# A state-space and Fourier kernel: angles reduced to one turn at the parameters, an exponential of degree 6, and six of its steps on ScalarE

## The chip, the cores and the metric

The kernel runs on one core of a Trainium2 chip. The engines are called as the profile calls them: PE (TensorE, with PEld for its weight loads), DVE (VectorE), ACT (ScalarE), POOL (GpSimd) and SP (SyncE, which issues most transfers). The metric is the device time of one execution in microseconds (us).

## The reference

Two independent layers are computed from fp32 inputs and laid side by side. A is a Fourier mixing layer, written as matrix products. B is a diagonal state-space layer: a kernel of 2048 taps is built from exponentials of complex numbers and convolved with the input by Fourier transforms of twice the length.

```python
# A: x is 2048 x 512
a = einsum("bsd,ed->bse", x, dft_hid_re)
b = einsum("bsd,ed->bse", x, dft_hid_im)
y = einsum("ts,bse->bte", dft_seq_re, a) - einsum("ts,bse->bte", dft_seq_im, b)
# B: u is 2048 x 512, N = 128 states for each of 512 channels
dt = exp(log_dt)
A = -exp(log_A_real) + 1j * A_imag
C = (C_real + 1j * C_imag) * dt[:, None]
P = exp((A * dt[:, None])[:, :, None] * pos[None, None, :])
K = 2.0 * einsum("dn,dnl->dl", C, P).real
y = irfft(rfft(u, 2L) * rfft(K, 2L), 2L)[:L] + u * D_skip
```

## The kernel before

All work is written as small processes (Python generators) that ask a planner for time on an engine, by `yield "dve", cost`, and then record their instructions. The planner simulates the engines with these costs and so sets, when the kernel is built, the one order in which each engine's instructions stand. On the chip each engine takes its list in that order and waits at an instruction whose data or buffer is not ready.

Layer A (class `Fnet`) is the bulk of PE's list. Each fp32 tile of 128 x 512 is split in two, a rounded part (`hi`, line 229, on ACT) and the rest (`lo`, line 234, on DVE), and three matmuls (line 378) make up one product; an item of the list is such a tile with its 12 matmuls. At the start the tiles of x are split too (`x_hi`, `x_lo`). So PE needs one instruction of ACT and one of DVE for every new tile, two of each for the first sixteen items.

Layer B (class `Ssm`) is spread between these matmuls. Channels go in 16 blocks of `CHUNK` = 32:

- `setup` and `setup_rest` make the parameters of the first 128 channels and of the other 384. Each calls `exp` (an exponential from plain DVE instructions: clamp, reduce by a multiple of ln 2, a Horner polynomial, and a power of two made by writing (k + 127) * 2^23 as an integer), and then `params`, which multiplies by dt. `par[:, 1]` is the angle of one step in turns. The first call works in tiles named `cs`, the second in tiles named `t`; the parameters lie in `xk_sb`.
- `seed_args` makes 11 seeds of a block: the exponent and the angle times 1, 2, 4, ... 1024 (lines 659 and 661, ACT), the angle rounded to whole turns (663, ACT) and reduced (665, DVE), clamped to half a turn (667, DVE), its absolute value (669, ACT), and an exponential and three sines on ACT with two loads of ACT's function tables (671 to 677).
- `seeds`, `tables1` and `tables2` turn them into tables of powers by complex products on DVE (lines 616, 625, 639, 645, with squares on ACT in line 632), the longest share of DVE's list. A block's `taps` are matmuls (line 812).
- `stage1_k` (line 861) and `stage1_u` (line 916) are first stages of the transforms of taps and input; their results leave PSUM through ACT and DVE (lines 846 to 850 and 926 to 930). `product` (1040, 1067) multiplies the spectra and starts the inverse, and `inverse` and `inverse2` (1161, 1139) end it.

Layer B's matmuls use two PSUM tiles called `f`, each handed on only when ACT and DVE have emptied it. The next `seed_args` starts when the one before is done, so its steps stand spread over the whole time of a block.

Of the kernel before, what the change touches and what calls it, by code (L numbers as in the profile page):

```python
# [10 lines left out]
I32 = mybir.dt.int32  # L11
AF = mybir.ActivationFunctionType
OP = mybir.AluOpType
# [5 lines left out]
RND = 1.5 * 2.0 ** 23  # L19
TWO_PI = 6.283185  # L20
LN2_HI = 0.693359375
LN2_LO = 0.693147180559945309 - LN2_HI


def fft_constants():
# [162 lines left out]
def act(cols):  # L188
    return 0.09 + cols * 0.00085


def dve(cols, rate=1.0):
    return (66 + cols / rate) / 960


def load(kb, rate=330):
    return max(0.55, kb / rate)
# [241 lines left out]
class Ssm:  # L439
# [63 lines left out]
    def exp(self, x, k, f, p):  # L503

        n = math.prod(x.shape[1:])
        v = self.nc.vector
        yield "dve", dve(n, 2)
        v.tensor_scalar(x, x, -87.0, 88.0, op0=OP.max, op1=OP.min)
        yield "dve", dve(n, 2)
        v.tensor_scalar(k, x, 1.0 / math.log(2.0), RND, op0=OP.mult, op1=OP.add)  # L510
        yield "dve", dve(n, 2)
        v.tensor_scalar(k, k, RND, None, op0=OP.subtract)
        yield "dve", dve(n)
        v.scalar_tensor_tensor(f, k, -LN2_HI, x, op0=OP.mult, op1=OP.add)
        yield "dve", dve(n)
        v.scalar_tensor_tensor(f, k, -LN2_LO, f, op0=OP.mult, op1=OP.add)
        yield "dve", dve(n, 2)
        v.tensor_scalar(p, f, 1.0 / 5040, None, op0=OP.mult)
        for c in (1.0 / 720, 1.0 / 120, 1.0 / 24, 1.0 / 6, 0.5, 1.0):
            yield "dve", dve(n)  # L520
            v.scalar_tensor_tensor(p, p, c, f, op0=OP.add, op1=OP.mult)
        yield "dve", dve(n, 2)
        v.tensor_scalar(f.bitcast(I32), k, 127.0, 2.0 ** 23, op0=OP.add, op1=OP.mult)
        yield "dve", dve(n)
        v.scalar_tensor_tensor(x, p, 1.0, f, op0=OP.add, op1=OP.mult)

# [28 lines left out]
            nc.sync.dma_start(self.all[:, i, FIRST:], self.nd[i, :, FIRST:])  # L555
        self.plan.set(self.in2_ev)

    def params(self, par, alpha, dt):

        v = self.nc.vector  # L560
        n = par.shape[2]
        yield "dve", dve(n), *APART
        v.tensor_tensor(par[:, 0], alpha, dt, op=OP.mult)
        yield "dve", dve(n), *APART
        v.scalar_tensor_tensor(par[:, 1], par[:, 1], 1.0 / (2 * math.pi), dt, op0=OP.mult, op1=OP.mult)
        yield "dve", dve(n), *APART
        v.tensor_tensor(par[:, 2], par[:, 2], dt, op=OP.mult)
        yield "dve", dve(n), *APART
        v.scalar_tensor_tensor(par[:, 3], par[:, 3], -1.0, dt, op0=OP.mult, op1=OP.mult)

    def setup(self):
        yield self.in_ev
        yield from self.exp(*self.tmp)
        x = self.tmp[0]
        self.plan.spawn(self.spread_dt(x[:, 2 * FIRST:]), 0)
        yield self.in1_ev
        yield from self.params(self.all[:, :, :FIRST], x[:, FIRST:2 * FIRST], x[:, :FIRST])

    def spread_dt(self, dt):

# [8 lines left out]
    def setup_rest(self):  # L589
        yield self.in2_ev  # L590
        dt, *t = self.tmp2
        par = self.all[:, :, FIRST:]
        yield from self.exp(par[:, 0], *t)
        yield self.dt_ev
        yield from self.params(par, par[:, 0], dt)
        self.plan.put(self.t1s)
        yield "dma", load(900)
        self.nc.sync.dma_start(self.par_dram, par)
        self.plan.set(self.par_ev)
# [47 lines left out]
    def seed_args(self, ck, box, ev):  # L647

        a, v = self.nc.scalar, self.nc.vector
        if CHUNK * ck >= FIRST:  # L650
            yield from self.load_par(ck)
        par = self.par[ck]
        yield self.res
        s = self.tab.tile([128, 3, 11, CHUNK], F32, name="seed")
        args = s[:, 0:3:2]
        e, k, r = (s[:, n] for n in range(3))
        n = 11 * CHUNK
        yield "act", act(2 * n) + 4 * act(0)
        a.activation(args[:, :, 0], par[:, 0:2], AF.Copy)
        for j in (1, 2, 4, 8):  # L660
            a.activation(args[:, :, j:min(2 * j, 11)], args[:, :, 0:min(j, 11 - j)], AF.Copy, scale=2.0 ** j)
        yield "act", act(n)
        a.activation(k, r, AF.Copy, bias=RND)
        yield "dve", dve(n)
        v.scalar_tensor_tensor(r, k, RND, r, op0=OP.subtract, op1=OP.subtract)
        yield "dve", dve(n, 2)
        v.tensor_scalar(r, r, 0.5, -0.5, op0=OP.min, op1=OP.max)
        yield "act", act(n)
        a.activation(k, r, AF.Abs)
        yield "act", act(n) + 1.3  # L670
        a.activation(e, e, AF.Exp, scale=-1.0)
        yield "act", act(6 * CHUNK) + 1.4
        a.activation(r[:, 0:6], r[:, 0:6], AF.Sin, scale=-TWO_PI)
        yield "act", act(5 * CHUNK)
        a.activation(r[:, 6:11], r[:, 6:11], AF.Sin, scale=TWO_PI)
        yield "act", act(n)
        a.activation(k, k, AF.Sin, scale=-TWO_PI, bias=self.halfpi)
        box.append(s)
        self.plan.set(ev)
# [494 lines left out]
CHUNK, FIRST, JOIN = 32, 128, 0  # L1174
# [79 lines left out]
```

## Time and profile before

| | |
|---|---|
| Median of 3 runs | 578.7 us (577.9 to 579.09) |
| Profiled execution, its own time | 577.28 us |
| Its span, first to last instruction | 575.5 us |
| ACT's splits (line 229) waiting for PE's matmuls | 52.0 us in 39 waits |
| DVE's splits (line 234) waiting for ACT's | 23.8 us in 14 waits |
| ACT table loads | 32, of 1.28 us |
| DMA moved | 133.70 MB, 232 GB/s |

The granted TensorE clock is at its full value in all slices of the span. The page's busy time of PE is of little use by itself, because matmuls overlap: a row of line 378 lasts some 0.39 us while the next one starts 0.23 us after it. So PE is read by the steps between starts, and a group of matmuls of one line (a burst) by its whole length. DVE's rows overlap by less, some 0.08 us.

### The profile page before, as it was taken

The page shows a single profiled execution, that of the slowest core. Times are in us where ns is not written, and L with a number is a line of the kernel's source. Part 1 is how long each engine was busy: PE and PEld are TensorE (multiplying, and loading weights), DVE is VectorE, ACT ScalarE, POOL GpSimd, SP SyncE. Part 2 cuts the span into 40 slices and gives each one's busy share as a digit, 9 for nine tenths or more (in the row PEclk, how much of TensorE's full clock was granted, in tenths as well). Part 3 has the DMA queues.
Part 4 walks back from the last instruction along what each step waited for, and adds up shares of the span by engine and source line. Part 5 has one row for each costly group of instructions (what it writes and reads, how often), then busy time and mean ns, then how long its engine had stood idle before and what let it go on. Part 6 is the DMA issues. An engine that isn't in the chain of part 4 may idle for free.

```text
span 575.5 us, 15666 instructions
## 1 busy us (share of the span) xinstructions
PE 567.4 (99%) x6278; PEld 433.0 (75%) x6278; DVE 522.5 (91%) x927; ACT 371.4 (65%) x728; POOL 40.2 (7%) x60
## 2 busy tenths in 40 slices
PE   8999999999999999999999999999999999999997
PEld 6777777788777777778787777777687778776685
DVE  7999999999999999999999999999998999547732
ACT  5779665663777495758669576754588845355623
POOL 0000000000110000100100100001100000000000
PEclk9999999999999999999999999999999999999999
DMA  8998999997459767866697889559998897599984
GB/s 272 325 372 256 280 286 276 283 278 179 128 156 234 193 179 232 202 165 220 171 259 211 221 202 259 137 153 254 293 298 239 225 294 227 131 281 266 274 233 147
DMA packets 147976, 133.70 MB, mean 232 GB/s; under 512 B 47296, under 2 KB 107328, under 8 KB 147648
## 3 DMA queue, kind: packets, MB, share of 16 engines
q1 hardware_dynamic: 138976, 115.54, 66.6%
q0 software_dynamic: 8064, 14.68, 12.7%
q10 hardware_dynamic: 864, 2.49, 1.8%
q8 instruction: 49, 0.80, 0.6%
q14 instruction: 23, 0.19, 0.1%
HBM read 89.95 MB, written 42.73 MB: 231 GB/s over the span
## 4 chain that ended last, share of the span: by engine, by line
PE 56%; DVE 34%; issue 6%; ACT 2%; DMA 1%; DVEq 0%; ACTq 0%
PE acc L378 45%; DVE prod L616 12%; DVE t L625 7%; DVE lo L234 5%; PE f L1040 3%; PE f L812 2%; PE f L1067 2%; DVE t L645 2%; PE f L916 2%; DVE cs L686 1%; DVE z L1024 1%; DVE uk L1026 1%; DVE t L639 1%; DVE xk_sb L848 1%; PE f L1139 1%
## 5 line engine op out<-in xcount | busy, mean ns | idle before, releaser
L378 PE MATMUL acc<-hi,x_hi 128*128 128x512 f32 x640 | 258.0, 403 | 0.0
L378 PE MATMUL acc<-lo,x_hi 128*128 128x512 f32 x640 | 250.2, 391 | 0.0
L378 PE MATMUL acc<-hi,x_lo 128*128 128x512 f32 x640 | 249.6, 390 | 0.0
L616 DVE TENSOR_TENSOR prod<-t,cs 128x1024 f32<-128x1024 f32 (+4 forms) x192 | 163.0, 867 | 1.7 <-ACT t L734 0.6
L378 PEld LDWEIGHTS acc<-hi,x_hi 128*128 128x128 f32 x640 | 120.2, 188 | 49.1 <-issue 23.8
L378 PEld LDWEIGHTS acc<-hi,x_lo 128*128 128x128 f32 x640 | 120.3, 188 | 26.0
L378 PEld LDWEIGHTS acc<-lo,x_hi 128*128 128x128 f32 x640 | 120.4, 188 | 23.0 <-DVE lo L234 0.2
L229 ACT ACTIVATE hi<-raw 128x512 fp32r<-128x512 f32 x132 | 82.6, 628 | 67.7 <-PE acc L378 52.0
L234 DVE TENSOR_TENSOR lo<-raw,hi 128x512 fp32r<-128x512 f32 x132 | 90.0, 684 | 23.9 <-ACT hi L229 23.8
L625 DVE TENSOR_TENSOR t<-prod 128x512 f32<-128x512 f32 (+4 forms) x192 | 94.1, 511 | 1.0
L632 ACT ACTIVATE square<-t 128x256 f32<-128x256 f32 (+1 forms) x64 | 36.7, 574 | 31.5 <-DVE t L625 28.9
L332 POOL DMA_DIRECT2D lo<-in_sT x28 | 24.3, 868 | 216.0 <-ACT lo L330 40.4
L1019 ACT ACTIVATE uk<-f 128x1024 f32<-128x1024 f32 x32 | 31.1, 1017 | 10.4 <-PE f L1040 7.5
L812 PEld LDWEIGHTS f<-t,t 128*32 128x32 f32 x2048 | 29.5, 110 | 7.2 <-issue 5.1
L399 ACT ACTIVATE y<-acc 128x512 f32<-128x512 f32 x47 | 27.9, 595 | 10.6 <-PE acc L378 10.5
L812 PE MATMUL f<-t,t 128*32 128x64 f32 x2048 | 32.4, 220 | 1.2 <-issue 0.7
L327 POOL DMA_DIRECT2D hi<-in_sT x28 | 16.1, 576 | 186.1 <-PE acc L378 147.6
L1024 DVE TENSOR_TENSOR z<-uk 128x512 f32<-128x512 f32 x32 | 21.9, 684 | 4.4 <-ACT uk L1019 2.9
L1082 ACT ACTIVATE z<-f 128x512 f32<-128x512 f32 x32 | 17.7, 592 | 11.6 <-PE f L1067 11.6
L645 DVE TENSOR_TENSOR t<-square 128x128 f32<-128x128 f32 (+1 forms) x64 | 24.6, 385 | 0.0
L1040 PE MATMUL f<-xt,w 64*32 64x256 f32 x768 | 23.5, 379 | 0.0
L1026 DVE TENSOR_TENSOR uk<-uk 128x512 f32<-128x512 f32 x32 | 22.1, 691 | 0.9
(100 smaller groups left out, 502.4 us busy)
## 6 DMA issues: line engine op xcount, KB each, us to landing
raw<-in_sT SPq DMA_DIRECT2D x99, 256.0 KB, 5.3
p<-y SPq DMA_DIRECT2D x32, 256.0 KB, 3.7
xk<-xk_sb SPq DMA_DIRECT2D x32, 256.0 KB, 5.4
zs<-z SPq DMA_DIRECT2D x32, 256.0 KB, 4.1
raw<-p SPq DMA_DIRECT2D x32, 256.0 KB, 4.9
hi<-in_sT POOLq DMA_DIRECT2D x28, 256.0 KB, 4.8
lo<-in_sT POOLq DMA_DIRECT2D x28, 256.0 KB, 5.1
xt<-xu SPq DMA_DIRECT2D x24, 256.0 KB, 4.5
```

Source lines behind the costliest of these rows:

```text
L229: self.nc.scalar.activation(hi, src, AF.Copy)
L234: self.nc.vector.tensor_tensor(lo, src, hi.bitcast(F32), op=OP.subtract)
L378: nc.tensor.matmul(acc[d], l[:, cols], r, start=k == 0 and n == 0, stop=k == len(items) - 1 and n == 2)
L399: self.nc.scalar.activation(y, ps, AF.Copy, scale=-1.0 if g[2] == 1 else 1.0)
L616: self.nc.vector.tensor_tensor(p.rearrange("p k d c m -> p k (d c) m"), src.rearrange("p d c l -> p (d c) l")[:, None, :, rows].to_broadca ...
L625: self.nc.vector.tensor_tensor(dst[:, :, :, rows], p[:, 0], p[:, 1, :, ::-1], op=OP.add)
L632: self.nc.scalar.activation(sq, t[:, :, :, m // 2:m], AF.Square)
L645: self.nc.vector.tensor_tensor(t[:, :, 0, m:2 * m:2], box[0][:, :, 0], box[0][:, :, 1], op=OP.subtract)
L812: nc.tensor.matmul(ps[32 * j:32 * j + 32, i], t1[:, d, c], t2[:, d, c], start=c == 0, stop=c == 1, tile_position=(0, 32 * j))
L1019: a.activation(uk[:, r].rearrange("p g c n d -> p g (c n d)"), p, AF.Copy)
L1026: v.tensor_tensor(t[:, r], t[:, r], u[:, r, :, ::-1], op=OP.mult)
L1040: nc.tensor.matmul(got[r][1][32 * xx:32 * xx + 32, g, 256 * c:256 * c + 256], self.w2[rows, 2 * q + r, xx, 32 * c:32 * c + 32], xt[rows].r ...
```

## The change

The change has three parts.

1. `params` reduces the angle of a step to half a turn up or down, once for each channel and state: a rounding on ACT (copy with the rounding constant as bias), and a subtraction and a clamp on DVE. Since whole turns stay whole when they are doubled, `seed_args` then leaves out its own clamp and reduces 10 of the 11 seeds (320 columns instead of 352). The sign of the reduced angle is turned, and the sign of the sines' scale with it.
2. The polynomial of `exp` has degree 6 instead of 7, with fitted coefficients: one Horner step less.
3. In `exp`, the polynomial's first product and the power of two are made on ACT, the second by a copy whose output is converted to an integer.

The requests to the planner (`yield`) stay as they were, also where their instruction has gone or moved, so the planner sets the order from the same costs.

```diff
+EXP = 0.00138146, 0.00836872, 0.04166839, 0.16666521, 0.49999993, 1.0
     def exp(self, x, k, f, p):
...
         v.scalar_tensor_tensor(f, k, -LN2_LO, f, op0=OP.mult, op1=OP.add)
         yield "dve", dve(n, 2)
-        v.tensor_scalar(p, f, 1.0 / 5040, None, op0=OP.mult)
-        for c in (1.0 / 720, 1.0 / 120, 1.0 / 24, 1.0 / 6, 0.5, 1.0):
+        a.activation(p, f, AF.Copy, scale=EXP[0])
+        for c in EXP[1:]:
             yield "dve", dve(n)
             v.scalar_tensor_tensor(p, p, c, f, op0=OP.add, op1=OP.mult)
+        yield "dve", dve(n)
         yield "dve", dve(n, 2)
-        v.tensor_scalar(f.bitcast(I32), k, 127.0, 2.0 ** 23, op0=OP.add, op1=OP.mult)
+        a.activation(f.bitcast(I32), k, AF.Copy, scale=2.0 ** 23, bias=127.0 * 2.0 ** 23)
...
-    def params(self, par, alpha, dt):
+    def params(self, par, alpha, dt, k):
...
         v.scalar_tensor_tensor(par[:, 1], par[:, 1], 1.0 / (2 * math.pi), dt, op0=OP.mult, op1=OP.mult)
+        a.activation(k, par[:, 1], AF.Copy, scale=-1.0, bias=RND)
...
         v.scalar_tensor_tensor(par[:, 3], par[:, 3], -1.0, dt, op0=OP.mult, op1=OP.mult)
+        v.scalar_tensor_tensor(par[:, 1], k, RND, par[:, 1], op0=OP.subtract, op1=OP.add)
+        v.tensor_scalar(par[:, 1], par[:, 1], 0.5, -0.5, op0=OP.min, op1=OP.max)
...
     def seed_args(self, ck, box, ev):
...
-        a.activation(k, r, AF.Copy, bias=RND)
+        a.activation(k[:, 1:], r[:, 1:], AF.Copy, scale=-1.0, bias=RND)
         yield "dve", dve(n)
-        v.scalar_tensor_tensor(r, k, RND, r, op0=OP.subtract, op1=OP.subtract)
+        v.scalar_tensor_tensor(r[:, 1:], k[:, 1:], RND, r[:, 1:], op0=OP.subtract, op1=OP.add)
         yield "dve", dve(n, 2)
-        v.tensor_scalar(r, r, 0.5, -0.5, op0=OP.min, op1=OP.max)
...
-        a.activation(r[:, 0:6], r[:, 0:6], AF.Sin, scale=-TWO_PI)
+        a.activation(r[:, 0:6], r[:, 0:6], AF.Sin, scale=TWO_PI)
         yield "act", act(5 * CHUNK)
-        a.activation(r[:, 6:11], r[:, 6:11], AF.Sin, scale=TWO_PI)
+        a.activation(r[:, 6:11], r[:, 6:11], AF.Sin, scale=-TWO_PI)
```

Line numbers after the change are larger: by 2 up to `exp`, by 3 at its end, by 6 or 7 from `seed_args` on. The new instructions are lines 520 and 526 (in `exp`), 570, 575 and 576 (in `params`).

The lists of PE, SP and POOL are the same rows in the same order. On DVE 22 rows go and 4 come, on ACT 6 come, and what stays keeps its order. Three places show it. The first is DVE's list at the end of the first exponential and through the first `params`, before the change (`cs` holds the exponential's values, `xk_sb` the parameters):

```order
L521 SCALAR_TENSOR_TENSOR cs<-cs 128x260
L234 TENSOR_TENSOR lo<-raw,hi 128x512
L234 TENSOR_TENSOR x_lo_247<-uk,x_hi_246 128x512
L523 TENSOR_SCALAR cs<-cs 128x260
L234 TENSOR_TENSOR lo<-raw,hi 128x512
L525 SCALAR_TENSOR_TENSOR cs<-cs 128x260
L563 TENSOR_TENSOR xk_sb<-cs 128x128
L565 SCALAR_TENSOR_TENSOR xk_sb<-xk_sb,cs 128x128
L567 TENSOR_TENSOR xk_sb<-xk_sb,cs 128x128
L569 SCALAR_TENSOR_TENSOR xk_sb<-xk_sb,cs 128x128
```

and the same place of DVE's list after it:

```order
L236 TENSOR_TENSOR lo<-raw,hi 128x512
L236 TENSOR_TENSOR x_lo_247<-uk,x_hi_246 128x512
L236 TENSOR_TENSOR lo<-raw,hi 128x512
L528 SCALAR_TENSOR_TENSOR cs<-cs 128x260
L566 TENSOR_TENSOR xk_sb<-cs 128x128
L568 SCALAR_TENSOR_TENSOR xk_sb<-xk_sb,cs 128x128
L572 TENSOR_TENSOR xk_sb<-xk_sb,cs 128x128
L574 SCALAR_TENSOR_TENSOR xk_sb<-xk_sb,cs 128x128
L575 SCALAR_TENSOR_TENSOR xk_sb<-cs,xk_sb 128x128
L576 TENSOR_SCALAR xk_sb<-xk_sb 128x128
```

The Horner step and the power of two (lines 521 and 523) have gone from between the splits, and the reduction and the clamp of the angle stand at the end.

The second is ACT's list at the same time, before the change, from the last split ahead of the first block's seeds (`seed`) to the first behind them:

```order
L229 ACTIVATE hi<-raw 128x512
L659 ACTIVATE seed<-xk_sb 128x2x32
L661 ACTIVATE seed<-seed 128x2x32
L661 ACTIVATE seed<-seed 128x2x64
L661 ACTIVATE seed<-seed 128x2x128
L661 ACTIVATE seed<-seed 128x2x96
L229 ACTIVATE x_hi_291<-uk 128x512
```

and after it:

```order
L231 ACTIVATE hi<-raw 128x512
L526 ACTIVATE cs<-cs 128x260
L570 ACTIVATE cs<-xk_sb 128x128
L666 ACTIVATE seed<-xk_sb 128x2x32
L668 ACTIVATE seed<-seed 128x2x32
L668 ACTIVATE seed<-seed 128x2x64
L668 ACTIVATE seed<-seed 128x2x128
L668 ACTIVATE seed<-seed 128x2x96
L231 ACTIVATE x_hi_291<-uk 128x512
```

The power of two and the rounding of the angle now stand between that split and the seeds; line 666 reads the clamped angle, so it stands behind line 576 of DVE.

The third is DVE's list between the reduction of the first block's seeds and the next step of the second exponential (`t` holds its values), before the change:

```order
L665 SCALAR_TENSOR_TENSOR seed<-seed 128x352
L234 TENSOR_TENSOR x_lo_323<-uk,x_hi_322 128x512
L234 TENSOR_TENSOR lo<-raw,hi 128x512
L667 TENSOR_SCALAR seed<-seed 128x352
L516 SCALAR_TENSOR_TENSOR t_166<-t_166 128x384
L234 TENSOR_TENSOR x_lo_350<-uk,x_hi_349 128x512
```

and after it:

```order
L672 SCALAR_TENSOR_TENSOR seed<-seed 128x320
L236 TENSOR_TENSOR x_lo_322<-uk,x_hi_321 128x512
L236 TENSOR_TENSOR lo<-raw,hi 128x512
L518 SCALAR_TENSOR_TENSOR t_166<-t_166 128x384
L236 TENSOR_TENSOR x_lo_352<-uk,x_hi_351 128x512
```

The clamp of the seeds is gone; ACT's next step for them (line 669 before, 675 after) now follows the reduction, two splits earlier in DVE's list.

More of the change, by code (lines that the diff above doesn't have):

```diff
@@ L505, in exp @@
         n = math.prod(x.shape[1:])
-        v = self.nc.vector
+        a, v = self.nc.scalar, self.nc.vector
         yield "dve", dve(n, 2)
@@ L556, in load_tables @@
         self.plan.set(self.in2_ev)
-    def params(self, par, alpha, dt):
-        v = self.nc.vector
+    def params(self, par, alpha, dt, k):
+        a, v = self.nc.scalar, self.nc.vector
         n = par.shape[2]
@@ L576, in setup @@
         yield self.in1_ev
-        yield from self.params(self.all[:, :, :FIRST], x[:, FIRST:2 * FIRST], x[:, :FIRST])
+        yield from self.params(self.all[:, :, :FIRST], x[:, FIRST:2 * FIRST], x[:, :FIRST], x[:, FIRST:2 * FIRST])
     def spread_dt(self, dt):
@@ L594, in setup_rest @@
         yield self.dt_ev
-        yield from self.params(par, par[:, 0], dt)
+        yield from self.params(par, par[:, 0], dt, t[0])
         self.plan.put(self.t1s)
```

## The prediction

> **What bounds the kernel now.** First the page's busy times: they show two engines that are almost never idle.
>
> ```profile
> PE 567.4 (99%) x6278; PEld 433.0 (75%) x6278; DVE 522.5 (91%) x927; ACT 371.4 (65%) x728; POOL 40.2 (7%) x60
> ```
>
> PE is busy 99% of the span and DVE 91%. A table of stretches (per row: the stretch, its length, then busy time and instructions of PE, PEld, DVE, ACT and POOL, the granted TensorE clock, DMA share, GB/s) separates them:
>
> ```profile
> 25.00:425.00 400.00, 397.73 (x4366) 303.68 (x4365) 395.99 (x702) 275.37 (x557) 38.58 (x54) 1.00 0.81 226
> ...
> 475.00:567.00 92.00, 92.00 (x1136) 68.96 (x1135) 57.64 (x89) 42.13 (x67) 0.00 (x0) 1.00 0.80 224
> ```
>
> From 25 to 425 us DVE is busy 395.99 of 400 us: its list runs without a hole. From 475 us on it is busy 57.64 of 92, and PE still 92.00. The clock is 1.00 in both. Whether PE is working or merely shown as busy is read from the steps between its starts, in the timeline of PE (start, length):
>
> ```profile
> 57.23 0.39 PE L378 MATMUL acc<-hi,x_lo 128*128 128x512 f32 x1
> 57.55 1.11 PE L916 MATMUL f<-xt,f1u 32*64 32x512 f32 x16
> ...
> 479.02 0.39 PE L378 MATMUL acc<-lo,x_hi 128*128 128x512 f32 x1
> 479.25 0.39 PE L378 MATMUL acc<-hi,x_lo 128*128 128x512 f32 x1
> ```
>
> From one 512-column matmul to the next PE takes 0.23 us at 479 us, where DVE has spare time, and the burst of line 916 starts 0.32 us after the last matmul at 57 us and lasts 1.11. The first 99 matmuls of the kernel, quoted further down from the chain, take 23.52 us or 0.238 each with the waits of the start; PE keeps this pace whether DVE is full or half idle. So PE is the bound, and its list can get shorter in time only where it waits. The rows in which a burst or a step is longer than its like are these:
>
> ```profile
> 69.69 1.36 PE L916 MATMUL f<-xt,f1u 32*64 32x512 f32 x16
> ...
> 95.33 1.35 PE L916 MATMUL f<-xt,f1u 32*64 32x512 f32 x16
> ...
> 154.18 1.10 PE L812 MATMUL f<-t,t 128*32 128x64 f32 x64
> 155.65 1.10 PE L812 MATMUL f<-t,t 128*32 128x64 f32 x64 [0.37 <-DVE t L625]
> ...
> 162.06 0.39 PE L378 MATMUL acc<-hi,x_lo 128*128 128x512 f32 x1
> 163.03 1.12 PE L861 MATMUL f<-ks,f1k 32*64 32x256 f32 x32 [0.58 <-DVE ks L835]
> ...
> 191.10 1.49 PE L1067 MATMUL f<-uk,ia 32*64 32x256 f32 x32
> ...
> 208.86 0.39 PE L378 MATMUL acc<-hi,x_lo 128*128 128x512 f32 x1
> 209.48 1.20 PE L1067 MATMUL f<-uk,ia 32*64 32x256 f32 x32 [0.23 <-DVE uk L1057]
> ...
> 232.06 1.78 PE L1067 MATMUL f<-uk,ia 32*64 32x256 f32 x32
> ...
> 314.28 1.45 PE L1067 MATMUL f<-uk,ia 32*64 32x256 f32 x32
> ...
> 325.50 1.99 PE L812 MATMUL f<-t,t 128*32 128x64 f32 x128
> ...
> 336.55 1.50 PE L1067 MATMUL f<-uk,ia 32*64 32x256 f32 x32
> ...
> 372.89 1.12 PE L1067 MATMUL f<-uk,ia 32*64 32x256 f32 x32
> ```
>
> Without a wait a burst of line 812 lasts 1.99 (325.50), of line 1067 1.12 (372.89), of line 916 1.11. The excess is therefore, in us: 0.25 at 69.69, 0.24 at 95.33, 0.58 at 154.18 (155.65 + 1.10 − 154.18 − 1.99), 0.65 at 162.06 (a step of 0.97 instead of 0.32), 0.37 at 191.10, 0.30 at 208.86 (0.62 instead of 0.32), 0.66 at 232.06, 0.33 at 314.28, 0.38 at 336.55: 3.76 us together. Two smaller ones, near 113 and 329 us, I don't count. Three of the rows name DVE as the releaser. The list of waits names it for line 1067 as well, and the timeline of DVE shows, inside the bursts at 95.33 and 232.06, the end of the DVE instruction that empties the PSUM bank:
>
> ```profile
> PEld f L1067 <- DVE uk L1060: 1.6, 4, 0.6
> ```
>
> ```profile
> 231.90 0.69 DVE L850 TENSOR_TENSOR xk_sb<-f,xk_sb 128x512 f32<-128x512 f32 x1
> ```
>
> ```profile
> 94.75 0.69 DVE L930 TENSOR_TENSOR zl<-f,zl 128x512 f32<-128x512 f32 x1
> ```
>
> These end at 95.44 and 232.59, and PE goes on just behind; I take 69.69 and 336.55 to be of the same two kinds. Two other long bursts have no DVE end in them, and I leave them as they are (0.59 and 0.87 us over 1.11):
>
> ```profile
> 46.85 1.70 PE L916 MATMUL f<-xt,f1u 32*64 32x512 f32 x16
> ...
> 76.64 1.98 PE L916 MATMUL f<-xt,f1u 32*64 32x512 f32 x16
> ```
>
> So DVE, always busy, is late for PE some ten times before 340 us and never after that. A shorter DVE list is worth what it takes out of these 3.76 us, not its own length.
>
> **What goes from DVE.** The clamp of the seed angles (line 667) goes, 16 times between 25 and 445 us:
>
> ```profile
> L667 DVE TENSOR_SCALAR seed<-seed x16: 331/334/339, 25.4 to 445.4; 128x352 f32<-128x352 f32 x16
> ```
>
> DVE starts its next instruction before this one's end:
>
> ```profile
> 25.45 0.33 DVE L667 TENSOR_SCALAR seed<-seed 128x352 f32<-128x352 f32 x1
> 25.70 0.55 DVE L516 SCALAR_TENSOR_TENSOR t<-t 128x384 f32<-128x384 f32 x1
> ```
>
> The step is 25.70 − 25.45 = 0.25 us, 0.08 less than the row's length. The rounding step (line 665) loses 32 of 352 columns; at the 0.33 us of 352 columns that is about 0.03 for 32. Each seed block thus frees 0.28 us, and 16 free 4.48. In both exponentials three instructions go: the first product (518), one Horner step (521) and the power of two (523), over 260 columns (cs) and over 384 (t):
>
> ```profile
> L521 DVE SCALAR_TENSOR_TENSOR t<-t 128x384 f32<-128x384 f32 x6 | 3.3, 556 | 0.2
> ...
> L521 DVE SCALAR_TENSOR_TENSOR cs<-cs 128x260 f32<-128x260 f32 x6 | 2.5, 424 | 0.1
> ...
> L518 DVE TENSOR_SCALAR t<-t 128x384 f32<-128x384 f32 x1 | 0.3, 348 | 0.0
> ...
> L523 DVE TENSOR_SCALAR cs<-cs 128x260 int32<-128x260 f32 x1 | 0.3, 285 | 0.0
> ```
>
> Lines 518 and 523 have the same form, so I give both of them 0.285 and 0.348. Less 0.08 each: 0.205 + 0.344 + 0.205 and 0.268 + 0.476 + 0.268, 1.77 us in all.
>
> **What comes to DVE.** Two instructions in each call of params, over 128 and 384 columns: one with two tensor inputs, like line 565, and a clamp, like lines 485 and 518.
>
> ```profile
> L565 DVE SCALAR_TENSOR_TENSOR xk_sb<-xk_sb,t 128x384 f32<-128x384 f32 x1 | 0.6, 551 | 0.0
> ...
> L565 DVE SCALAR_TENSOR_TENSOR xk_sb<-xk_sb,cs 128x128 f32<-128x128 f32 x1 | 0.3, 283 | 0.0
> ...
> L485 DVE TENSOR_SCALAR dskip<-dskip 128x128 f32<-128x128 f32 x1 | 0.2, 220 | 0.0
> ```
>
> Each reads what the one ahead wrote, so I count full lengths: 0.283 + 0.220 + 0.551 + 0.348 = 1.40 us. The net relief is 1.77 − 1.40 + 4.48 = 4.85 us, of which 0.37 has been gained when the parameters are done and the rest comes in sixteen steps of 0.28, one every 28 us.
>
> **What comes to ACT.** Six copies with scale and bias, of 260, 384, 260, 384, 128 and 384 columns, at first the like of this one:
>
> ```profile
> L663 ACT ACTIVATE seed<-seed 128x352 f32<-128x352 f32 x16 | 7.8, 490 | 0.2
> ```
>
> By 0.490 us for 352 columns they cost at most 0.55 each, some 3 us, and ACT is busy 275.37 of the 400 us. Two of them write integers; no row of ACT does that. The nearest row is line 523 on DVE, which writes integers in 0.285 us as line 663 writes floats on ACT, without any visible extra, so I take nothing extra; the other end would be a multiple of 0.49, and nothing below zero is possible for an instruction that is added. All six stand before 45 us. The place where they can hurt is the first call of params, where ACT waits for DVE already:
>
> ```profile
> 19.25 0.26 ACT L659 ACTIVATE seed<-xk_sb 128x64 f32<-128x64 f32 x1 [2.41 <-DVE xk_sb L565]
> ```
>
> Line 659 will wait for the new clamp instead of line 565. DVE comes there 0.75 us earlier (0.205 + 0.344 + 0.205), then runs the rows that used to follow line 565 and the two new ones; the rounding on ACT lies beside lines 567 and 569. I get a start of line 659 about 0.2 us later. Behind it in ACT's queue stand the splits of the input for PE, and these have cover:
>
> ```profile
> 22.00 0.68 DVE L234 TENSOR_TENSOR lo<-raw,hi 128x512 fp32r<-128x512 f32 x1
> ```
>
> ```profile
> 4.55 23.52 PE acc L378 x99
> ```
>
> That DVE row completes the eighth item at 22.68 us. PE has 99 matmuls from 4.55 to 28.07, 12 per item, so the eighth item starts 15 matmuls before 28.07, at 24.67 with 0.227 each. The cover is 2.0 us; 0.2 us costs nothing.
>
> A rule of the Trainium skill speaks against these moves: "ScalarE: Activation LUTs", section Rules for kernel authors, gives plain multiplications, additions, minima and maxima to VectorE because it does them faster per element. The rows agree on the speed (0.490 us here against 0.334 for the same 352 columns on DVE). By that rule the four moved instructions would stay on DVE, the relief would be 0.95 us smaller and the forecast about 0.9 us later; the stretch table is what decides otherwise, since ACT has 125 us free there and DVE none.
>
> **The sum.** I keep a ledger of DVE's lead. Before 191 us it has gained 0.37 + 6 × 0.28 = 2.05, and the waits up to 162 us need 1.72: they go, one after the other. Up to 232 us it has 0.37 + 8 × 0.28 = 2.61; the waits ahead of that one sum to 2.39, so 0.22 of its 0.66 goes. By 336 us the lead is 0.37 + 12 × 0.28 = 3.73, and the last two (0.71) go as well: 2.61 + 0.71 = 3.32 us. What DVE gains after that is idle time, because PE no longer waits for it. The removed clamp lies in the chain to ACT too, and that helps ACT, which is not waited for at these places. PE's, SP's and POOL's lists are unchanged. The span of the profiled execution is 575.5 us, its own time 577.28, and the median of the three runs 578.7, 1.4 above it. 577.28 − 3.3 gives 574.0 for a run like the profiled one, and 578.7 − 3.3 = **575.4 us** for a median.
>
> **Rivals.**
> *The lead is spent on the way* (0.22). DVE's order is still that of a plan that counts the removed instructions. If DVE arrives early at data that ACT or PE deliver at their old time, its lead shrinks before PE's next wait. Against it: DVE has no such wait in 400 us, so it does not stand close behind its suppliers often. If half of the ledger is lost, 1.7 us remain: 577.0. If only the waits up to 95 us go (0.49), the time is 578.2.
> *DVE alone sets the pace* (0.08). Then its whole relief comes out: 578.7 − 4.85 = 573.9. It needs 1.1 us of waits that I did not give to DVE, such as the two bursts at 46.85 and 76.64 (1.46). Against it stands the step of 0.23 us that PE keeps where DVE is half idle. The Trainium skill's "Perfetto Trace Analysis", section Identifying the Most-Contended Engine, would have it so: it does not count matmul busy time as nearness to the limit but the share of weight loads, here 75% against DVE's 91%; by the constant step this trace doesn't agree.
> *It doesn't shorten what PE waits for* (0.06). The moved copies come back to DVE as waits (lines 523, 528 and 575 of the changed kernel each wait for ACT), the early lead is used up, and the single steps of 0.28 come too late for the waits before 170 us: 578.2 to 578.9.
> *Slower* (0.06). ACT's copies into integers or their waits hold the splits behind them. From 2.0 us late on, PE waits in full. If these copies took 5 us longer at 17 us and again in the second exponential, PE would lose 3 us twice; 578.7 + 6 − 3.3 = 581.4. Against it: the same number of table loads on ACT and the integer row on DVE.
>
> **How the numbers follow.** The forecast as such has 0.58, with 574.3 to 576.6. A change of 0.2% (1.2 us, to 577.5) is about what a measurement of this kernel can tell from none. Faster by more: 0.58 + 0.08 + 0.12 from the first rival = 0.78; within: 0.10 + 0.06 = 0.16; slower by more: 0.06. The range must leave out no more than 0.2: from 573.2 (the whole relief and half of the two bursts, 578.7 − 4.85 − 0.7) to 577.9 (a fifth of the ledger).
>
> **What would show it.** In the changed profile DVE's busy time should be some 6.7 us lower (16 × 0.334 and 16 × 0.033 for the seeds, 2.25 − 1.40 for the rest, by the rows' lengths), ACT's 2 us higher; the bursts named above should have 1.12 and 1.99 us; DVE should now have waits between 100 and 425 us; the former line 659, now 666, should start between 19.2 and 19.6 us. The prediction is wrong if DVE stays without waits and PE's bursts still are long, or if PE waits for ACT's splits before 45 us.

## The result, and the profile after

| | before | changed |
|---|---|---|
| Median of 6 runs each | 579.12 us (577.9 to 579.61) | 575.79 us (574.38 to 576.28) |
| Ratio, 95% interval | | 0.994 [0.9924, 0.9956] |
| Profiled execution | 577.28 us | 576.01 us |
| Its span | 575.5 us | 574.2 us |

The changed kernel is faster by 3.3 us or 0.6%. The two profiled executions are only 1.3 us apart: that of before (577.28 us) was shorter than all six runs of its kernel, and runs of one kernel differ by some 2 us. So the medians give the size, and the traces show the places.

The page's busy times of the changed kernel:

```profile
PE 566.7 (99%) x6278; PEld 432.7 (75%) x6278; DVE 518.5 (90%) x909; ACT 374.9 (65%) x734; POOL 40.3 (7%) x60
```

DVE has 4.0 us less than before (522.5), ACT 3.5 more (371.4). The table of stretches of the changed kernel (columns as before):

```profile
25.00:425.00 400.00, 398.39 (x4374) 304.58 (x4373) 395.59 (x693) 281.14 (x565) 38.65 (x54) 1.00 0.82 228
475.00:567.00 92.00, 92.00 (x1135) 68.99 (x1134) 56.18 (x87) 41.94 (x68) 0.00 (x0) 1.00 0.79 223
```

DVE is as full as it was (395.99 before): where the clamps have gone, the rest of its list has moved up. What changed is PE, 397.73 before and 398.39 now. The chain that ended last, first on the page of before, then on that of the changed kernel, says the same by share of the span:

```profile
PE 56%; DVE 34%; issue 6%; ACT 2%; DMA 1%; DVEq 0%; ACTq 0%
```

```profile
PE 88%; DVE 7%; issue 2%; ACT 1%; DMA 1%; DVEq 0%
```

Traced back from the end, the chain now stays on PE for most of the way and crosses to DVE for 7% instead of 34%. The places themselves stand in PE's timeline of the changed kernel (start, length; lines 818, 867, 922 and 1073 are the former 812, 861, 916 and 1067):

```profile
47.47 2.14 PE L922 MATMUL f<-xt,f1u 32*64 32x512 f32 x16
...
70.76 1.11 PE L922 MATMUL f<-xt,f1u 32*64 32x512 f32 x16
...
77.47 1.95 PE L922 MATMUL f<-xt,f1u 32*64 32x512 f32 x16
...
96.14 1.17 PE L922 MATMUL f<-xt,f1u 32*64 32x512 f32 x16
...
154.82 2.03 PE L818 MATMUL f<-t,t 128*32 128x64 f32 x128
...
162.14 0.40 PE L380 MATMUL acc<-hi,x_lo 128*128 128x512 f32 x1
163.12 1.12 PE L867 MATMUL f<-ks,f1k 32*64 32x256 f32 x32 [0.58 <-DVE ks L841]
...
191.13 1.31 PE L1073 MATMUL f<-uk,ia 32*64 32x256 f32 x32
...
208.71 0.39 PE L380 MATMUL acc<-hi,x_lo 128*128 128x512 f32 x1
209.03 1.20 PE L1073 MATMUL f<-uk,ia 32*64 32x256 f32 x32
...
231.60 1.78 PE L1073 MATMUL f<-uk,ia 32*64 32x256 f32 x32
...
313.64 1.12 PE L1073 MATMUL f<-uk,ia 32*64 32x256 f32 x32
...
335.46 1.12 PE L1073 MATMUL f<-uk,ia 32*64 32x256 f32 x32
```

Read beside the rows of before, the starts of the same bursts differ by +0.62 us (47.47 against 46.85), +1.07 (70.76), +0.81 (96.14), +0.64 (154.82), +0.03 (191.13), −0.15 (the matmul at 208.71), −0.46 (231.60), −0.64 (313.64) and −1.09 (335.46); the last burst is also 0.38 shorter. This execution lost 1.07 us ahead of 70 us, and from there to 337 us it gained about 2.5, some 2.2 of it at the places that the prediction lists: the excess at 69.69, 154.18, 208.86, 314.28 and 336.55 is gone but for 0.04 us, that at 95.33 went from 0.24 to 0.06 and that at 191.10 from 0.37 to 0.19. Two have stayed: 0.66 at 162.14 and 0.66 at 231.60.

The loss at the start begins before any changed instruction can act. At PE's first burst of line 922 it is 0.37 us (28.37 against 28.00): the first matmuls of layer A start 0.42 to 0.43 us apart instead of 0.23, two steps of that kind in the execution of before and four here. This start differs from execution to execution: the same burst stands between 27.60 us (`e2`, below) and 28.75 us (`e8`) in the kernels with this order of PE's list. Of the rest, 0.25 us are lost at the burst at 37.25 us and 0.44 at that of 47.47, where PE waits for DVE. DVE was late there, and its input had come late. ACT's timeline of the changed kernel, where line 520 (11.38 us) is the first new instruction:

```profile
9.94 0.64 ACT L231 ACTIVATE x_hi<-uk 128x512 fp32r<-128x512 f32 x1 [1.45 <-DMA uk<-in_x]
...
14.77 0.63 ACT L231 ACTIVATE hi<-raw 128x512 fp32r<-128x512 f32 x1 [2.23 <-DMA raw<-in_sT]
...
18.50 0.41 ACT L526 ACTIVATE cs<-cs 128x260 int32<-128x260 f32 x1
20.22 0.31 ACT L570 ACTIVATE cs<-xk_sb 128x128 f32<-128x128 f32 x1 [1.31 <-DVE xk_sb L568]
21.15 0.26 ACT L666 ACTIVATE seed<-xk_sb 128x64 f32<-128x64 f32 x1 [0.62 <-DVE xk_sb L576]
```

Transfers of the input held the split at 9.94 us for 1.45 us (0.86 before) and that at 14.77 us for 2.23 (1.57 before). DVE's rows show what a late start does later: its line 936, which empties a PSUM bank, starts at 47.70 us, and the same row of before at 46.63. A full list passes a late start on, until something takes it up. Why the transfers were late is not shown.

### The profile page after: what moved, and what is told of

Same layout as the page of the kernel before. It is cut to its first block, busy times and chain, and to the rows that moved or that the text cites. A ratio compares the mean times of both kernels' runs of the same rounds, so it can differ in the third digit from the quotient of the medians.

```text
span 574.2 us, 15643 instructions
## 1 busy us (share of the span) xinstructions
PE 566.7 (99%) x6278; PEld 432.7 (75%) x6278; DVE 518.5 (90%) x909; ACT 374.9 (65%) x734; POOL 40.3 (7%) x60
## 4 chain that ended last, share of the span: by engine, by line
PE 88%; DVE 7%; issue 2%; ACT 1%; DMA 1%; DVEq 0%
PE acc L380 69%; PE f L1046 5%; PE f L818 5%; PE f L1073 3%; DVE prod L623 2%; DVE t L632 2%; PE f L867 1%; DVE lo L236 1%; PE f L1167 1%; PE f L922 1%; PE f L1145 1%; DMA out_yb<-zl 1%; DMA raw<-in_sT 1%; DVE zl L934 0%; DVE t L652 0%
## 5 line engine op out<-in xcount | busy, mean ns | idle before, releaser
L1025 ACT ACTIVATE uk<-f 128x1024 f32<-128x1024 f32 x32 | 31.1, 1018 | 10.8 <-PE f L1046 9.0
```

The source lines that it names most:

```text
L1025: a.activation(uk[:, r].rearrange("p g c n d -> p g (c n d)"), p, AF.Copy)
```

## The experiments

The theory to be tested, called D: what counts is the length of DVE's list in the stretch from 25 to 340 us, because DVE is late for PE there; sixteen clamps are nearly all of it. Its first rivals say that the gain comes from the start (exponentials and parameters), or from ACT's seeds, which are ready earlier without the clamp in their chain; others stand with the later runs. The first four kernels ran beside each other on one chip, the next four likewise; the median of before was 578.63 us both times.

**The changed kernel once more** (`e0_after_again`), without an edit.

> The changed kernel once more, to have it beside the parts on one chip. Both theories: 3.0 to 3.6 us below the kernel before (ratio 0.994 to 0.995). The spread of single executions of both kernels is some 2 us.

Measured: 575.65 us, ratio 0.9951 [0.9938, 0.9964].

**Only the clamps out** (`e1_clamp_out`): the kernel of before without line 667.

```diff
         yield "dve", dve(n, 2)
-        v.tensor_scalar(r, r, 0.5, -0.5, op0=OP.min, op1=OP.max)
```

> The kernel before with only the 16 clamps of the seed angles left out; exponential and parameters as before. Theory D (PE waits for DVE, and DVE's list is shorter): relief 16 x 0.25 = 4.0 us, of which the ledger lets 2.0 count by 232 us and 3.0 by 336 us: 3.0 us below the kernel before. Rival S (the early part, exponential and parameters, makes the gain): 0 to 0.3 us below it.

Measured: 575.08 us, 0.9941 [0.9928, 0.9954]. This is the whole gain, by one line. The page's busy times:

```profile
PE 565.8 (99%) x6278; PEld 432.6 (75%) x6278; DVE 519.0 (91%) x911; ACT 372.0 (65%) x728; POOL 40.2 (7%) x60
```

**The clamps back** (`e2_clamp_back`): the changed kernel with the clamp and the 32 columns restored.

```diff
-        a.activation(k[:, 1:], r[:, 1:], AF.Copy, scale=-1.0, bias=RND)
+        a.activation(k, r, AF.Copy, scale=-1.0, bias=RND)
...
-        v.scalar_tensor_tensor(r[:, 1:], k[:, 1:], RND, r[:, 1:], op0=OP.subtract, op1=OP.add)
+        v.scalar_tensor_tensor(r, k, RND, r, op0=OP.subtract, op1=OP.add)
...
+        v.tensor_scalar(r, r, 0.5, -0.5, op0=OP.min, op1=OP.max)
```

> The changed kernel with the reduction over all 352 columns and the clamp of the seeds put back; the exponential and params stay changed. Theory D: relief 0.37 us, so 0 to 0.5 us below the kernel before. Rival S: 3 us below it.

Measured: 579.21 us, 1.0009 [0.9999, 1.0019]. The new exponential, the copies on ACT and the reduction in `params` are worth nothing that can be measured. PE's timeline of this kernel has the waits again, at the same places and of the same size as before:

```profile
154.21 1.10 PE L819 MATMUL f<-t,t 128*32 128x64 f32 x64
155.68 1.10 PE L819 MATMUL f<-t,t 128*32 128x64 f32 x64 [0.37 <-DVE t L632]
...
314.37 1.42 PE L1074 MATMUL f<-uk,ia 32*64 32x256 f32 x32
...
336.67 1.45 PE L1074 MATMUL f<-uk,ia 32*64 32x256 f32 x32
```

**A clamp that nobody waits for** (`e3_clamp_aside`): the changed kernel, with the clamp on a tile of its own that nothing reads, made once at the start. The chain of the seeds stays as short as in the changed kernel; only DVE's time is spent.

```diff
+        self.scr = self.const.tile([128, 11 * CHUNK], F32, name="scr")
+        nc.vector.memset(self.scr, 0.25)
...
+        v.tensor_scalar(self.scr, self.scr, 0.5, -0.5, op0=OP.min, op1=OP.max)
```

> The changed kernel with a clamp of the same size put back at the same place of DVE's list, on a scratch tile that nothing reads: DVE's length is back, the chain of the seeds stays short (ACT waits for the reduction alone). Theory D: relief 0.85 us, 0.5 to 0.9 us below the kernel before. Rival A (the gain comes from ACT, which no longer waits 11.3 us for the clamp): about 3 us below it, like the changed kernel.

Measured: 578.31 us, 0.9998 [0.9988, 1.0008]: the gain is gone. Of the 0.5 to 0.9 us that D still expected of the rest of the relief the medians show 0.3. So it is DVE's length and not ACT's earlier seeds, and that rival falls. The busy times of this kernel's page:

```profile
PE 567.1 (98%) x6278; PEld 432.9 (75%) x6278; DVE 522.3 (91%) x926; ACT 374.1 (65%) x734; POOL 40.2 (7%) x60
```

**How far down it goes** (`e4_no_reduce`): the changed kernel without line 672.

```diff
-        v.scalar_tensor_tensor(r[:, 1:], k[:, 1:], RND, r[:, 1:], op0=OP.subtract, op1=OP.add)
```

> The changed kernel with the reduction of the seeds to one turn (line 672) left out as well, so the sines get angles of many turns; DVE loses 16 more steps of 0.40 us, 6.4 us in all. Theory D with PE as the floor: only PE's waits for DVE that are left can go, in the changed profile those near 111, 157, 191, 209 and 232 us, 1.7 us, and what of the one at 47 us is DVE's: 1.2 to 2.5 us below the changed kernel, about 573.5. Rival P (DVE alone sets the pace, to the end): 6 us below the changed kernel, about 569.5.

Measured: 573.45 us, 0.9915 [0.99, 0.993]. DVE loses another 5.8 us (from 518.5), the time only 2.2 (from the 575.65 of `e0`). On this kernel's page and in its table of stretches, PE has become the limit and DVE has holes (392.93 of 400):

```profile
PE 564.5 (99%) x6278; PEld 432.7 (76%) x6278; DVE 512.7 (90%) x893; ACT 373.9 (65%) x734; POOL 40.2 (7%) x60
```

```profile
25.00:425.00 400.00, 399.57 (x4462) 307.22 (x4465) 392.93 (x681) 281.51 (x568) 38.55 (x54) 1.00 0.83 230
```

The list of DVE's waits from 25 to 425 us (in all, times, the longest) has four entries here; the longest two:

```profile
DVE z L933 <- ACT z L931: 1.0, 1, 1.0
DVE cs L691 <- ACT seed L682: 0.7, 1, 0.7
```

In the changed kernel the same list had one (and in `e2` and `e3`, with DVE's length back, 0.2 and 0.6 us in all):

```profile
DVE seed L672 <- ACT seed L670: 0.2, 1, 0.2
```

**How far up it goes** (`e5_three_aside`): the changed kernel with three such clamps aside in each block.

```diff
+        v.tensor_scalar(self.scr, self.scr, 0.5, -0.5, op0=OP.min, op1=OP.max)
+        v.tensor_scalar(self.scr, self.scr, 0.5, -0.5, op0=OP.min, op1=OP.max)
+        v.tensor_scalar(self.scr, self.scr, 0.5, -0.5, op0=OP.min, op1=OP.max)
```

> The changed kernel with three clamps per block on a scratch tile that nothing reads: 16 x 3 x 0.25 = 12.0 us more on DVE, 7.2 more than the kernel before. Theory D: DVE has no slack from 25 to 425 us and PE waits for it one for one: 6 to 8 us above the kernel before, about 585.5. Rival C (DVE's work is covered by PE's list in this stage, and only the clamp's place in the seeds' chain counts): within 1 us of the kernel before.

Measured: 590.93 us, 1.0213 [1.0199, 1.0228], 12.3 us over before. The size was missed twice over. First, three clamps on one tile cost more than 0.25 us each, since each needs the one ahead: the next one starts 0.37 and 0.38 us after it, and only the instruction behind the third 0.25 us after it. DVE's timeline of this kernel at the first three, and its busy times:

```profile
25.86 0.33 DVE L676 TENSOR_SCALAR scr<-scr 128x352 f32<-128x352 f32 x1
26.23 0.34 DVE L677 TENSOR_SCALAR scr<-scr 128x352 f32<-128x352 f32 x1
26.61 0.34 DVE L678 TENSOR_SCALAR scr<-scr 128x352 f32<-128x352 f32 x1
26.86 0.55 DVE L518 SCALAR_TENSOR_TENSOR t<-t 128x384 f32<-128x384 f32 x1
```

```profile
PE 571.9 (97%) x6278; PEld 433.7 (74%) x6278; DVE 533.3 (91%) x958; ACT 375.2 (64%) x734; POOL 40.2 (7%) x60
```

DVE is 10.8 us longer than before instead of 7.2. Second, PE came back slowly from one of its stops; PE's timeline, then the stretch behind it (the clock is the number after POOL's):

```profile
46.74 1.09 PE L927 MATMUL f<-xt,f1u 32*64 32x512 f32 x8
49.04 1.09 PE L927 MATMUL f<-xt,f1u 32*64 32x512 f32 x8 [1.21 <-ACT lo L332]
50.06 0.66 PE L380 MATMUL acc<-hi,x_hi 128*128 128x512 f32 x1
50.51 0.63 PE L380 MATMUL acc<-lo,x_hi 128*128 128x512 f32 x1
```

```profile
49.90:53.40 3.50, 3.50 (x12) 2.67 (x9) 3.46 (x10) 1.63 (x4) 0.32 (x1) 0.55 0.91 173
```

From 50.51 on a matmul takes 0.43 us from start to start instead of 0.23; over the eight or so until 53.4 us that is 1.6 us. 10.8 + 1.6 = 12.4, and 12.3 was measured. That the two simply add is not shown, because DVE worked on through the slow stretch (3.46 of 3.50 us). Upward, DVE's length counts at least one for one, and rival C falls.

**The planner told** (`e6_replanned`): the changed kernel with requests that fit its instructions: those of the moved steps go to ACT, the clamp's and the Horner step's are gone, and `params` has three more. **And with the clamp alone** (`e7_clamp_out_replanned`): before without the clamp and without its request. In both the order of every engine's list is another. The core of the two edits:

```diff
-        yield "dve", dve(n, 2)
+        yield "act", act(n)
...
-        yield "dve", dve(n, 2)
```

```diff
-        yield "dve", dve(n, 2)
-        v.tensor_scalar(r, r, 0.5, -0.5, op0=OP.min, op1=OP.max)
```

> The changed kernel with the planner told of the change: requests for ACT's time where steps went to ACT, none where an instruction has gone, two more in params. The order of all engines is then another one. Theory D: the same DVE length, so 2 to 4.5 us below the kernel before; with a better fit between lists up to 1 us below the changed kernel. Rival O (the order matters more than the relief): outside of that, either way.

> The kernel before with the clamp of the seeds and its request to the planner left out, nothing else; the order is planned anew. Theory D: 2.5 to 4.5 us below the kernel before, like the run without the clamp in the old order. Rival O: outside of that.

Measured: 581.2 us, 1.0048 [1.0032, 1.0063], and 594.46 us, 1.0275 [1.0257, 1.0293], with DVE at 518.0 and 519.9 us. Both have DVE's relief and are slower than before. The longest waits of PE behind its start in the first one name DVE and transfers at new places:

```profile
PE f L1074 <- DVE uk L1064: 2.0, 2, 1.8
...
PE f L1047 <- DMA p<-y: 1.2, 1, 1.2
```

In the second one, PE's timeline has a hole of 4.35 us and a slow return behind it:

```profile
446.62 0.39 PE L378 MATMUL acc<-hi,x_hi 128*128 128x512 f32 x1
451.36 0.80 PE L378 MATMUL acc<-lo,x_hi 128*128 128x512 f32 x1 [4.35 <-DMA lo<-in_sT]
451.95 0.63 PE L378 MATMUL acc<-hi,x_lo 128*128 128x512 f32 x1
```

A tile of layer A was loaded too late for its new place. Two more stops with such a return (1.09 us up to 99.85 and 3.36 us up to 531.25) stand in this trace. So these two orders cost more than the relief brings, and the changed kernel's gain depends on having kept the old one. What makes the old order better than these two was not tried.

**The reduction on another engine** (`e8_reduce_on_pool`): what `e4` left out, done in full by ACT and GpSimd; the sum is kept.

```diff
-        v.scalar_tensor_tensor(r[:, 1:], k[:, 1:], RND, r[:, 1:], op0=OP.subtract, op1=OP.add)
+        a.activation(k[:, 1:], k[:, 1:], AF.Copy, bias=-RND)
+        self.nc.gpsimd.tensor_tensor(r[:, 1:], k[:, 1:], r[:, 1:], op=OP.add)
```

> The changed kernel with the reduction of the seeds' angles (line 672, 320 columns, 0.488 us, 16 times) taken off DVE: ScalarE makes the negative whole number by one more copy, and GpSimd adds it to the angle. All of the computation is kept. Theory D (DVE's length counts until PE's own length is reached, which the run without the reduction put at 573.45): DVE loses 16 x 0.488 = 7.8 us and ScalarE, with room, gains 16 x 0.46, so about 573.5. Rival G (GpSimd and VectorE get in each other's way): DVE's other rows become longer and the time stays at 575.8 or above, with DVE busy falling by less than 5 us. Rival Q (GpSimd's queue): the additions stand in one queue with 56 transfers whose issue waits 5 to 41 us for a free tile (135.5 us for PE in all); an addition that comes late by that much makes the seeds late, and the time goes above 579, with waits of DVE for the seeds.

Measured: 580.57 us beside 579.11 for before, 1.0029 [1.0015, 1.0043]. Sixteen rows of 0.49 us have left DVE, and its busy time has gone up, from 518.5 to 522.3:

```profile
PE 568.7 (98%) x6278; PEld 433.1 (75%) x6278; DVE 522.3 (90%) x893; ACT 378.6 (65%) x750; POOL 57.7 (10%) x76
```

`e4` has the same 893 DVE rows in the same order, and DVE busy for 512.7 us: beside it the list is 9.6 us longer. The timelines of POOL and DVE in this kernel show how:

```profile
153.26 1.52 POOL L673 TENSOR_TENSOR seed<-seed 128x320 f32<-128x320 f32 x1 [1.73 <-PE acc L380]
```

```profile
153.96 1.11 DVE L652 TENSOR_TENSOR t<-square 128x256 f32<-128x256 f32 x1
```

The DVE row of line 652 that starts while GpSimd is adding (153.26 to 154.78) takes 1.11 us; in the changed kernel such rows take 0.424 on the mean:

```profile
L652 DVE TENSOR_TENSOR t<-square 128x256 f32<-128x256 f32 x48 | 20.3, 424 | 0.0
```

Laid row by row beside `e4`, the sixteen DVE rows that start while an addition runs last 9.8 us longer together, and all the others 1.3. So the expectation that the two engines get in each other's way holds. Of the one that names GpSimd's queue the time came (above 579), but not the sign: DVE has no wait for the seeds on its list of waits here.

No kernel beat the changed one without leaving out a part of its computation. `e1`, which leaves the clamp of the seeds out, lies 0.57 us below `e0`, with intervals that overlap.

## Why the prediction was right, and where it was not

Set side by side, DVE's busy time and the measured time of the kernels that keep the order give one curve:

| kernel | DVE busy, us | time, us |
|---|---|---|
| `e4`, no reduction | 512.7 | 573.45 |
| changed, `e0` | 518.5 | 575.65 |
| `e1`, only the clamps out | 519.0 | 575.08 |
| `e3`, clamps aside | 522.3 | 578.31 |
| before (time on both chips) | 522.5 | 578.63 |
| `e2`, clamps back | 522.6 | 579.21 |
| `e5`, three aside | 533.3 | 590.93 |

Below 518 us of DVE a microsecond is worth 0.4 (2.2 of 5.8). Between the changed kernel and before it is 0.75 by `e0` (3.0 of 4.0) and 1.0 by `e1` (3.55 of 3.5), which the intervals (2.1 to 3.6 us and 2.7 to 4.2 us) do not tell apart. Above, it is more than one (12.3 of 10.8).

1. *PE keeps its pace, and DVE is late for it at some ten places before 340 us.* Right. `e2` shows the waits with the clamps, `e0` and `e1` have lost most of them, and `e4` shows the floor: with most waits gone a shorter DVE list brings little.

2. *The relief is 4.85 us, 4.48 of it from the clamps and the 32 columns.* Too large. DVE's busy time, in which overlapping rows count once, fell by 4.0 us, and by 3.5 for the clamps alone (`e1`), 0.22 each, though the step from a clamp to the next row is 0.25. The 6.7 us that the prediction expected of the busy time were the rows' lengths, overlaps and all: the wrong measure for it, as the step was right for the ledger.

3. *0.37 us is gained when the parameters are done.* It is not there: `e2`, which should have it, has DVE busy for 522.6 us (522.5 before) and is not faster. The 0.5 us between the changed kernel and `e1` (518.5 against 519.0) is what the 32 columns are worth: the step behind the reduction is 0.40 us instead of 0.43, sixteen times. Where the 0.37 went was not followed. The start of an execution shifts by more than that, 1.07 us in the profiled one.

4. *The ledger: waits up to 191 go, 0.22 of 0.66 at 232, all of it at 314 and 336, 3.32 us.* The mechanism holds, and the sum agrees with the 3.33 us between the medians. That it agrees so closely is luck, because the relief was too large (4.85 us against 4.0) and two of PE's waits were missing. In the trace the 0.65 us at 162 stayed, as did half of the 0.37 at 191 and all of the 0.66 at 232, and some 2.5 us were gained. Three traces with the clamps' length on DVE (575.5, 577.7 and 576.1 us of span) lie 2.7 us above three without it (574.2, 573.7, 573.2). Counted from the end of the burst at 46.85, which PE leaves behind DVE in all six, they lie 3.2 us apart (527.0, 529.1 and 527.4 us against 524.6, 524.4 and 525.0): the rest is the late start of two of the three without.

The prediction says that no DVE row ends inside the bursts at 46.85 and 76.64 us and leaves them out. That is a wrong reading. DVE's timeline of before:

```profile
46.63 0.68 DVE L930 TENSOR_TENSOR zl<-f,zl 128x512 f32<-128x512 f32 x1
...
76.70 0.69 DVE L930 TENSOR_TENSOR zl<-f,zl 128x512 f32<-128x512 f32 x1
```

These rows empty the PSUM bank and end at 47.31 and 77.39 us, and the bursts end 1.24 and 1.23 us later, as that at 95.33 does (1.24 after 95.44). In the changed kernel the first of the two is 0.44 us longer, because DVE comes to it later, and again ends 1.23 us behind the same row:

```profile
47.70 0.68 DVE L936 TENSOR_TENSOR zl<-f,zl 128x512 f32<-128x512 f32 x1
```

In `e1` this burst is 1.32 us long. The second stays at 1.95 us in the changed kernel, where PE and DVE both come to it 0.8 us later than before, and is 1.50 us long in `e4`. With their 0.59 and 0.87 us the waits come to 5.22 us. If DVE's measured 4.0 us are spread over sixteen blocks, 0.25 us each, the waits up to every place are more than the lead that DVE has there. All of the lead up to 336 us then counts, twelve of the sixteen steps: 12 x 0.25 = 3.0 us, an estimate from these figures. `e4` fits the larger sum of waits: it is 5.2 us below before, and these two bursts still have 0.30 and 0.39 us to lose there.

5. *DVE should now have waits between 100 and 425 us.* Wrong: one of 0.2 us came, and `e2` and `e3`, which have no relief, show 0.2 and 0.6 us. Less was gained than DVE needed, so it stayed behind PE. Longer waits come only in `e4`. The prediction would have been wrong by its own words if bursts had stayed long besides. Those at 162 and 232 us did; the excess of most others is gone.

6. *ACT's copies take at most 0.55 us, integers nothing extra, and cost nothing.* Right: 0.41 us for the 260 columns into integers, on the row of line 526 above, less than the 0.49 of 352 columns in floats. ACT's busy time rose by 3.5 us, nearer to the 3 of the sum than to the 2 named at the end. Line 666 started at 21.15 us, not between 19.2 and 19.6. That fits the late transfers: in `e2`, with waits for DVE at lines 570 and 666 as here (1.47 and 0.62 us there, 1.31 and 0.62 here), it started at 19.39 us. PE did not wait for a split because of it.
   The Trainium skill ("ScalarE: Activation LUTs", Rules for kernel authors) would have left these steps on VectorE, and the forecast put 0.9 us on that. `e1`, which leaves all of them there, is not slower than the changed kernel, so here the choice made no difference that these runs show. That ScalarE is slower per element agrees with the rows, which is no loss where it has 119 us free.

7. *The rivals.* DVE alone sets the pace: the change itself does not decide it, since `e1` gained as much as its DVE list lost. `e4` rules it out for a still shorter list (573.45 us, where this rival asked for 569.5), and `e5` bears it out for a longer one. The Trainium skill's "Perfetto Trace Analysis" (Identifying the Most-Contended Engine), which leaves matmul busy time out of the comparison, points at DVE; `e5` agrees with it from before upward, and `e4` does not below the changed kernel. The lead spent on the way: in part, at 162 and 232 us. Nothing gained, or slower by ACT: neither was seen. The run that came out slower did so through the order (`e6`, `e7`), which this change leaves alone.

## What to carry to other kernels

Where two engines are both full, price a shorter list by the waits that it can remove on the other engine, with its own length as the upper end, and expect a longer list to cost its full length. To find these waits, look for the row that ends a fixed time ahead of each long burst's end, in every burst, also in those whose waiting the list of waits does not show. A clamp on a scratch tile that nothing reads is a cheap way to ask whether an engine's time or a chain's length matters, before anything is rewritten. Where a planner sets the order, an edit that keeps the order and one that plans anew are two different changes, and the second can cost several times what the first gains.

## What the runs showed of the hardware

PE comes back slowly from some of its waits. After the 4.35 us at 446.62 in `e7_clamp_out_replanned` matmuls of line 378 start 0.43 us apart instead of 0.23, and the table of stretches gives the granted clock as half:

```profile
451.40:456.00 4.60, 4.60 (x11) 3.67 (x12) 4.60 (x7) 2.46 (x5) 0.00 (x0) 0.50 0.57 163
```

The same kind of return followed the wait of 1.21 us in `e5`, where the granted clock is 0.50 from 50.24 to 53.65 us and 1.00 in the 3.4 us on either side. None followed a wait of 1.23 us in the same kernel or the 1.77 us in `e6`, whose clock stays at 1.00; PE's rows behind these two waits:

```profile
161.10 1.10 PE L823 MATMUL f<-t,t 128*32 128x64 f32 x64 [1.23 <-DVE t L634]
```

```profile
536.17 1.20 PE L1074 MATMUL f<-uk,ia 32*64 32x256 f32 x32 [1.77 <-DVE uk L1064]
```

The pages of before and of the changed kernel show the clock as full from the first slice on, and yet PE's first matmuls of layer A stand 0.42 to 0.43 us apart. A slow return added 1.6 us (eight steps, 0.2 us each) in `e5`, and 2 us (ten steps) in `e7`. The Trainium skill ("TensorE: Matmul & The Clock Gate", Part 1: The HAM clock gate) halves the clock after about one idle window of 3.4 us, counted by windows that run freely, and gives it back after as much sustained work. The 4.35 us and the 3.41 us at half the clock in `e5` agree with that; that 1.21 us was enough here and 1.23 and 1.77 were not, by the rows, it does not explain. In `e5` the 3.41 us ahead of the drop (46.83 to 50.24) hold the stop and bursts of line 927, whose tiles are 32*64, and almost nothing else, while every 3.4 us around the other two stops hold matmuls with tiles of 128 rows (line 380, and line 823 in `e5`). Whether that decides was not tried.

GpSimd's addition over 128x320 holds VectorE up, 1.11 us instead of 0.424 for one row, and takes 1.08 us itself on the mean, 17.3 us for sixteen. Work whose removal from VectorE is worth 5.8 us (`e4`) made VectorE's other rows 9.6 us longer together when it was moved there (`e8`). The Trainium skill ("Perfetto Trace Analysis", Optimizing Scalar/DVE Operations) warns that these two engines share a port to SBUF, so that work moved between them might not help; this run agrees.

The step from a clamp of 352 columns (0.33 us long) to an independent instruction is 0.25 us, to one that needs its result 0.37 to 0.38 (`e5`): a row's length can overstate or understate what its removal frees.
